# Cosformer attention followed by a low-rank mixer MLP: q features of four batches transposed by DMA, attention units moved to other PSUM banks

## The chip, the cores and the metric

The kernel runs on one core of a Trainium2 chip. The time is that of one execution on the device, in microseconds, taken on the slowest core, which here is the only one. The profiled execution is a single run with the hardware profiler; its span is the time from its first to its last instruction. TensorE (PE in the profile) multiplies matrices; what it writes goes to PSUM, which has eight banks of 128 partitions by 2 KB. VectorE (DVE) and ScalarE (ACT) read PSUM and write SBUF; GpSimd (POOL) converts v and issues the stores of the output; SyncE (SP) issues the loads and the DMA transposes.

## The reference

q, k and v have 8 batches, 8 heads, 576 positions and 64 features each, in float32. Attention is linear: no softmax, but features `phi`, a state `kv` per head, and a denominator. Its output is the input of a mixer with a low-rank part over the positions and an MLP over the channels.

```python
def phi(x, c, s):
    r = np.maximum(x, 0.0)
    return np.concatenate([r * c, r * s], axis=-1)       # 64 features become 128
q_p, k_p = phi(q, cos_w, sin_w), phi(k, cos_w, sin_w)    # cos_w, sin_w by position
kv = np.einsum('bhsf,bhsd->bhfd', k_p, v)
z = np.sum(k_p, axis=2)
num = np.einsum('bhsf,bhfd->bhsd', q_p, kv)
den = np.einsum('bhsf,bhf->bhs', q_p, z)[..., None] + 1e-06
attn = num / den

x = attn.transpose(0, 2, 1, 3).reshape(8, 576, 512)
h = x.transpose(0, 2, 1) @ U @ V                         # U 576 x 32, V 32 x 576
u = x + h.transpose(0, 2, 1)
out = u + np.maximum(u @ w_ch1, 0.0) @ w_ch2             # 512 -> 2048 -> 512
```

## The kernel before

**Tiling.** The 576 positions of a batch are cut into four chunks of 128 (chunk `c` holds positions 4p + c) and a tail of 64 (`c` = 4). Tails of an even and an odd batch share one tile, in its lower and upper 64 rows (`tail(b)`), so the MLP treats two batches as a pair with a common tail. All products are bf16.

**Attention of one batch** is a row of units:

- `k_prep`, `q_prep`, `v_prep`: k, q and v from the float32 loads to bf16 features, on DVE, ACT and POOL. The features of q of one batch stand in `q_p` (one buffer, four chunks of 128 rows by 8 heads x 128 features) and `q_tl`.
- `qtr_unit(b, c)` (L250): eight TensorE transposes, one for each head, turn one chunk of `q_p` so that features lie on partitions; they write a PSUM tile `t_ps` with tag `T` (one buffer), and one copy on DVE (in batches 2 and 3 sometimes ACT) brings it to `q_pT` (one buffer) or `q_tlT`.
- `kv_unit(b, hg)` (L229): the state of four heads, 20 matmuls, PSUM tag `T`, a cast on DVE.
- `x_unit(b, c)` (L311): eight matmuls of `q_pT` with `kv`, PSUM tag `X` (two banks), a reciprocal and a product on DVE, giving `x_bf`.
- `A_unit(b)` (L338): five matmuls with U, PSUM tag `T`, a cast on DVE; `u_unit(b, c)` (L354): one matmul with V, PSUM tag `T`, an addition on DVE, giving `u_bf` or `u_tl`.
- `utr_dma` (L377): DMA transposes of u, two chunks at a time (a 128 x 1024 matrix), and of the pair's tail (128 x 512), issued by SP; they write `uT` and `uT_tl`.

**The MLP of a pair** is 72 slots: 16 of `g1_main` for the even batch, 16 for the odd one (each four matmuls of 512 columns into tag `g`, three banks, and a ReLU on ACT), 4 of `g1_tail`, and 36 of `g2_part` (each four matmuls into tag `o`, two banks; after every fourth slot DVE adds u and POOL or SP issues the store). The four pairs make 288 slots, numbered through: pair 1, with batches 2 and 3, has slots 72 to 143, and its slots from 108 on are `g2_part`. `g1_main` of an even batch starts at slots 0, 72, 144, 216, that of an odd one at 16, 88, 160, 232.

**What sets the order.** Everything is written out by hand: each engine runs its instructions in the order in which the program issues them. After slot i the list `todo[i]` adds attention units. `attention_plan(b)` (L527) gives the slots of one batch relative to a slot `w`: preparation from `p0` on, `qtr_unit` at -9 to -1, `kv_unit` at 0 and 2, `x_unit` at 4 to 12, `A_unit` at 14, `u_unit` at 16 to 20, `utr_dma` at 18 to 21, and the loads of batch b + 1 at `p0` + 1, + 2 and + 7. `w` is 40, 57, 88, 124, 160 and 196 for batches 2 to 7. So the attention of batches 4 and 5 runs beside pair 1's MLP, that of 6 and 7 beside pair 2's, and pair 3's has none beside it. Batches 0 and 1 are ordered separately ahead of and beside the first slots.

SP's queue holds, in order, the loads (for each of k, v and q a tail of 128 KB and a main part of 1 MB; `kst` has two buffers, `vst` and `qst` one each) and the transposes of u. ACT's holds `q_prep` and the ReLUs of `g1_main`, so `q_prep` of batch 6 stands ahead of the ReLU of slot 144.

Of the kernel before, what the change touches and what calls it, by code (L numbers as in the profile page):

```python
# [17 lines left out]
def kernel(  # L18
# [11 lines left out]
    nc = tc.nc  # L30
# [18 lines left out]
    def tail(b):  # L49
        lo = TS * (b % 2)  # L50
        return slice(lo, lo + TS)
# [49 lines left out]
    def cast(eng, o, i):  # L101
        if eng is nc.scalar:
            nc.scalar.activation(out=o, in_=i, func=AF.Copy, bias=0.0, scale=1.0)
        else:
            eng.tensor_copy(out=o, in_=i)  # L105
# [140 lines left out]
    def qT_alloc(b):  # L246
        if b not in q_pT:
            q_pT[b] = pool.tile([P, 4, H, P], BF16, tag="q_pT", bufs=1, name="q_pT")

    def qtr_unit(b, c, h0=0, h1=H, eng=None, tag="T", bufs=1):  # L250
        qT_alloc(b)
        t_ps = ps.tile([P, H, P], BF16, tag=tag, bufs=bufs, name="t_ps")
        for h in range(h0, h1):
            nc.tensor.transpose(  # L254
                out=t_ps[:, h, :],
                in_=q_p[b][:, c, h, :] if c < 4 else q_tl[:, h, :],
                identity=ident,
            )
# [265 lines left out]

    ORD = (4, 0, 1, 2, 3)

    def attention_plan(b):  # L527

        p0 = -26 if b % 2 == 0 and b > 2 else -14
        plan = [(p0, lambda: v_prep(b))]  # L530
        for n, c in enumerate(ORD):
            ke = (V_, A_) if b == 3 else (V_, V_)
            plan.append((p0 + n, lambda c=c, ke=ke: k_prep(b, c, ke)))
            if b == 2:
                plan.append((p0 + n, lambda c=c: q_prep(b, c, (V_, A_))))
            else:
                plan.append((p0 + n, lambda c=c: q_prep(b, c, (A_, None))))
                plan.append((p0 + n + 1, lambda c=c: q_prep(b, c, (None, A_))))
            ev = A_ if b in (2, 3) and n % 2 == 0 else V_
            plan.append((-9 + 2 * n, lambda c=c, ev=ev: qtr_unit(b, c, eng=ev)))  # L540
        plan.append((0, lambda: kv_unit(b, 0, "T", 1)))
        plan.append((2, lambda: kv_unit(b, 1, "T", 1)))
        for n, c in enumerate(ORD):
            plan.append((4 + 2 * n, lambda c=c: x_unit(b, c, "X", 1)))
        plan.append((14, lambda: A_unit(b, "T", 1)))
        for n, c in enumerate(ORD):
            plan.append((16 + n, lambda c=c: u_unit(b, c, "T", 1)))
        if b % 2 == 1:
            plan.append((18, lambda: utr_dma(b, 4, 5)))
        plan.append((19, lambda: utr_dma(b, 0, 2)))  # L550
        plan.append((21, lambda: utr_dma(b, 2, 4)))
# [102 lines left out]
    def put(at, thunk):  # L654
        todo.setdefault(at, []).append(thunk)

    put(17, lambda: uTt_direct(0, "o", 2, V_))
    for n, (b, c) in enumerate([(b, c) for b in range(2) for c in ORD]):
        put(18 + n, lambda b=b, c=c: u_unit(b, c, "T", 1))
    for n, t in enumerate(loads(2, nc.sync)):  # L660
        put((11, 12, 12)[n], t)
    for b, w in ((2, 40), (3, 57), (4, 88), (5, 124), (6, 160), (7, 196)):
        for o, t in attention_plan(b):
            put(w + o, t)
    for i, s in enumerate(slots):
        s()
        for t in todo.get(i, []):
# [31 lines left out]
```

## Time and profile before

| | us |
|---|---|
| median of 3 runs (lowest to highest) | 354.38 (351.99 to 355.33) |
| the profiled execution's own time | 352.06 |
| its span | 350.3 |
| TensorE busy, share of the span | 326.5, 93% |
| DVE busy / ACT busy / POOL busy | 165.8 / 150.5 / 52.2 |
| first matmul of pair 1's `g2_part` (slot 108) | 165.95 |

The granted TensorE clock is 0.994 over the span. The page lists busy time by engine, the chain of work that ended last, and groups of instructions by line; answers of the trace give the same for a stretch of the span. A matmul's duration in a row contains its fill, and matmuls overlap: the distance between starts, which the chain of waits shows, is what one adds to TensorE's time. An idle time in brackets stands behind the instruction that waited, with what released it.

### The profile page before, as it was taken

The page shows a single profiled execution, that of the slowest core. Times are in us where ns is not written, and L with a number is a line of the kernel's source. Part 1 is how long each engine was busy: PE and PEld are TensorE (multiplying, and loading weights), DVE is VectorE, ACT ScalarE, POOL GpSimd, SP SyncE. Part 2 cuts the span into 40 slices and gives each one's busy share as a digit, 9 for nine tenths or more (in the row PEclk, how much of TensorE's full clock was granted, in tenths as well). Part 3 has the DMA queues.
Part 4 walks back from the last instruction along what each step waited for, and adds up shares of the span by engine and source line. Part 5 has one row for each costly group of instructions (what it writes and reads, how often), then busy time and mean ns, then how long its engine had stood idle before and what let it go on. Part 6 is the DMA issues. An engine that isn't in the chain of part 4 may idle for free.

```text
span 350.3 us, 6126 instructions
## 1 busy us (share of the span) xinstructions
PE 326.5 (93%) x2537; PEld 177.0 (51%) x2565; DVE 165.8 (47%) x355; ACT 150.5 (43%) x257; POOL 52.2 (15%) x101
## 2 busy tenths in 40 slices
PE   7689999999787899999999989999999999999995
PEld 2464654475444345556455435556455444464443
DVE  5668444845745953244745852244745630001211
ACT  2967445856627025565707025565600036660000
POOL 6340503003113040000111440000111100000000
PEclk9899999999999999999999999999999999999999
DMA  8999999964752993000798591000312150001121
GB/s 214 263 279 260 213 238 244 280 180 152 201 159 61 239 299 64 2 2 0 165 314 275 141 283 44 2 0 2 90 67 56 60 135 2 0 2 55 65 92 60
DMA packets 58587, 46.03 MB, mean 131 GB/s; under 512 B 26720, under 2 KB 55680, under 8 KB 58560
## 3 DMA queue, kind: packets, MB, share of 16 engines
q1 hardware_dynamic: 51856, 33.82, 37.9%
q0 software_dynamic: 6704, 11.82, 13.6%
q8 instruction: 20, 0.33, 0.4%
q14 instruction: 7, 0.06, 0.1%
HBM read 36.86 MB, written 9.44 MB: 132 GB/s over the span
## 4 chain that ended last, share of the span: by engine, by line
PE 75%; DVE 9%; DMA 9%; issue 3%; POOL 2%; ACT 1%; SPq 0%; POOLq 0%; DVEq 0%
PE o_ps L481 29%; PE g_ps L431 28%; DMA vst<-in_v_dram 5%; PE gt_ps L449 4%; PE t_ps L254 4%; PE va_ps L361 3%; DMA vt<-in_v_dram 3%; DVE k_p L205 3%; PE kv_ps L237 2%; DVE o_sb L491 2%; PE x_ps L318 2%; PE a_ps L344 2%; DMA w_bf<-in_moe_w_ch_dram 2%; POOL v_ext L105 1%; DVE u_bf L362 1%
## 5 line engine op out<-in xcount | busy, mean ns | idle before, releaser
L438 ACT ACTIVATE hid<-g_ps 128x512 bf16<-128x512 f32 x128 | 76.3, 597 | 116.9 <-PE g_ps L431 116.9
L431 PE MATMUL g_ps<-uT,w_bf 128*128 128x512 bf16 x512 | 120.6, 379 | 0.4
L481 PE MATMUL o_ps<-w_bf,hid 128*128 128x512 bf16 (+1 forms) x510 | 116.9, 372 | 1.4 <-DVE o_sb L491 0.5
L481 PEld LDWEIGHTS <-hid 128*128 128x128 bf16 x528 | 49.5, 98 | 52.6 <-issue 2.8
L431 PEld LDWEIGHTS <-w_bf 128*128 128x128 bf16 x512 | 47.9, 98 | 54.7 <-issue 4.8
L491 DVE TENSOR_TENSOR o_sb<-u_bf,o_ps 128x512 f32<-128x512 bf16 (+1 forms) x33 | 22.1, 669 | 61.6 <-PE o_ps L481 61.6
L501 POOL DMA_DIRECT2D out_dram<-o_sb x24 | 13.4, 558 | 180.9 <-DVE o_sb L491 164.4
L105 DVE COPY q_pT<-t_ps 128x1024 bf16<-128x1024 bf16 (+1 forms) x25 | 16.7, 668 | 26.5 <-PE t_ps L254 24.9
L362 DVE TENSOR_TENSOR u_bf<-x_bf,va_ps 128x512 bf16<-128x512 bf16 x32 | 22.0, 687 | 15.1 <-PE va_ps L361 15.1
L203 ACT ACTIVATE q_p<-qst,sinw 128x512 bf16<-128x512 f32 (+1 forms) x36 | 23.3, 664 | 0.0
L254 PE MATMUL t_ps<-ident,q_p 128*128 128x128 bf16 x256 | 20.4, 223 | 2.9 <-DVE q_pT L105 0.9
L254 PEld LDWEIGHTS <-q_p 128*128 128x128 bf16 x256 | 17.2, 99 | 9.7 <-issue 3.6
L105 POOL CAST v_ext<-vst 128x512 bf16<-128x512 f32 (+1 forms) x32 | 17.3, 582 | 17.7 <-DMA vst<-in_v_dram 16.1
L205 DVE TENSOR_SCALAR k_p<-kst,cosw 128x512 bf16<-128x512 f32 (+1 forms) x36 | 17.9, 514 | 1.6 <-DMA kst<-in_k_dram 1.6
L328 DVE TENSOR_TENSOR x_bf<-x_ps,rec 128x512 bf16<-128x512 f32 x24 | 16.6, 691 | 0.8
L361 PE MATMUL va_ps<-A_sb,V_bf 128*128 128x512 bf16 x39 | 14.7, 377 | 1.7 <-DVE u_tl L362 0.9
L449 PE MATMUL gt_ps<-uT_tl,w_bf 128*128 128x128 bf16 x256 | 16.1, 219 | 0.0
L449 PEld LDWEIGHTS <-w_bf 128*128 128x128 bf16 x256 | 15.1, 98 | 1.4
L237 PEld LDWEIGHTS <-k_p 128*128 128x128 bf16 x256 | 11.2, 98 | 8.3 <-issue 2.5
L203 ACT ACTIVATE q_p<-qst,cosw 128x512 bf16<-128x512 f32 x20 | 14.2, 710 | 2.4 <-DMA qst<-in_q_dram 2.4
L237 PE MATMUL kv_ps<-v_ext,k_p 128*128 128x65 bf16 x256 | 12.5, 195 | 2.9 <-DVE u_bf L362 1.9
L105 DVE CAST kv<-kv_ps 128x260 bf16<-128x260 f32 x16 | 6.8, 428 | 17.5 <-PE kv_ps L237 17.4
(95 smaller groups left out, 265.0 us busy)
## 6 DMA issues: line engine op xcount, KB each, us to landing
kst<-in_k_dram SPq DMA_DIRECT2D x7, 1024.0 KB, 11.2
qst<-in_q_dram SPq DMA_DIRECT2D x7, 1024.0 KB, 11.3
vst<-in_v_dram SPq DMA_DIRECT2D x7, 1024.0 KB, 11.3
out_dram<-o_sb POOLq DMA_DIRECT2D x24, 256.0 KB, 4.5
w_bf<-in_moe_w_ch_dram POOLq DMA_DIRECT2D x8, 512.0 KB, 11.8
out_dram<-o_sb SPq DMA_DIRECT2D x7, 256.0 KB, 2.3
kst<-in_k_dram SPq DMA_DIRECT2D x2, 512.0 KB, 7.7
qst<-in_q_dram SPq DMA_DIRECT2D x2, 512.0 KB, 8.8
```

Of the source, the lines that this page charges most:

```text
L105: eng.tensor_copy(out=o, in_=i)
L203: nc.scalar.activation(out=o, in_=i, func=AF.Relu, bias=0.0, scale=w)
L205: eng.tensor_scalar(out=o, in0=i, scalar1=0.0, scalar2=w, op0=ALU.max, op1=ALU.mult)
L237: nc.tensor.matmul(out=acc[:, i, :], lhsT=k_p[b][:, c, h, :] if c < 4 else k_tl[:, h, :], rhs=vx[:, c, h, :], start=(c == 0), stop=(c == 4),)
L254: nc.tensor.transpose(out=t_ps[:, h, :], in_=q_p[b][:, c, h, :] if c < 4 else q_tl[:, h, :], identity=ident,)
L361: nc.tensor.matmul(out=va, lhsT=V_bf[:, c, :], rhs=A_sb[b], start=True, stop=True)
L362: nc.vector.tensor_tensor(out=u_bf[b][:, c, :] if c < 4 else u_tl[b // 2][rows, :], in0=x_of(b, c, rows), in1=va[rows, :], op=ALU.add,)
L431: nc.tensor.matmul(out=g_ps.rearrange("p (c t) -> p c t", c=4), lhsT=w1_bf[:, d, j * P : j * P + P], rhs=uT[b][:, :, d, :], start=(d == 0) ...
L438: nc.scalar.activation(out=hid[b][:, j, :], in_=g_ps, func=AF.Relu, bias=0.0, scale=1.0)
L449: nc.tensor.matmul(out=g_ps[:, jj, :], lhsT=w1_bf[:, d, j * P : j * P + P], rhs=uT_tl[pr][:, d, :], start=(d == 0), stop=(d == 3),)
L481: nc.tensor.matmul(out=o[:, cols], lhsT=lhs[:, j, c * P : c * P + P], rhs=w2_bf[:, j, cols], start=(j == 0), stop=(j == NJ - 1),)
L491: nc.vector.tensor_tensor(out=o_sb[:, cols], in0=u[:, cols], in1=o[:, cols], op=ALU.add)
```

## The change: three parts

First, the q features of batches 4 to 7 are no longer transposed by `qtr_unit` but by a new function, `qtr_dma`: three DMA transposes for a batch, issued by SP. One turns the tail (64 rows by 1024), two turn two chunks each (128 x 2048). They write `q_pT` and `q_tlT` directly. The loads of the next batch, which stand in the same queue, get other slots: in batch 4 they are at -6 to -4, in batches 5, 6 and 7 (the last has none) at `p0` + 9 to + 11, behind the q transposes at `p0` + 4, + 6 and + 8.

Second, `kv_unit`, `A_unit` and `u_unit` of batches 2 to 7 (and `u_unit` of batches 0 and 1) leave tag `T`. They take tag `o` in the 36 slots of a pair in which `g1` runs, and tag `g` in those in which `g2` runs; `spare` makes the choice. Tag `T` is left to the q transposes of TensorE.

Third, in the part ahead of the first slot, `den_unit(0, 4, 8)` is issued ahead of one `xh_unit` and the two `uTd_open`, where it stood behind them.

The core of the diff:

```diff
+    def qtr_dma(b, c0, c1):
+        qT_alloc(b)
+        if c0 < 4:
+            nc.sync.dma_start_transpose(
+                out=q_pT[b][:, c0:c1, :, :].rearrange("f c h t -> f (c h) t"),
+                in_=q_p[b][:, c0:c1, :, :].rearrange("p c h f -> p (c h f)"),
+            )
+        else:
+            nc.sync.dma_start_transpose(
+                out=q_tlT[:, :, tail(b)],
+                in_=q_tl[tail(b), :, :].rearrange("p h f -> p (h f)"),
+            )
...
-    def attention_plan(b):
+    Q_BY_DMA = (4, 5, 6, 7)
+
+    def spare(at):
+        return ("o", 2) if at % 72 < 36 else ("g", 3)
+
+    def attention_plan(b, w):
+        plan = []
+
+        def put(at, f, *a, tag=False):
+            if tag:
+                a = a + spare(w + at)
+            plan.append((w + at, lambda: f(b, *a)))
...
-            ev = A_ if b in (2, 3) and n % 2 == 0 else V_
-            plan.append((-9 + 2 * n, lambda c=c, ev=ev: qtr_unit(b, c, eng=ev)))
-        plan.append((0, lambda: kv_unit(b, 0, "T", 1)))
-        plan.append((2, lambda: kv_unit(b, 1, "T", 1)))
+            if b not in Q_BY_DMA:
+                ev = A_ if b in (2, 3) and n % 2 == 0 else V_
+                put(-9 + 2 * n, qtr_unit, c, 0, H, ev)
+        lo = (p0 + 1, p0 + 2, p0 + 7)
+        if b in Q_BY_DMA:
+            q0 = (-18, -16, -8) if b == 4 else (p0 + 4, p0 + 6, p0 + 8)
+            for at, (c0, c1) in zip(q0, ((4, 5), (0, 2), (2, 4))):
+                put(at, qtr_dma, c0, c1)
+            lo = (-6, -5, -4) if b == 4 else (p0 + 9, p0 + 10, p0 + 11)
+        put(0, kv_unit, 0, tag=True)
+        put(2, kv_unit, 1, tag=True)
...
-        plan.append((14, lambda: A_unit(b, "T", 1)))
+            put(16 + n, u_unit, c, tag=True)
+        put(14, A_unit, tag=True)
...
-            for at, t in zip((p0 + 1, p0 + 2, p0 + 7), loads(b + 1, nc.sync)):
-                plan.append((at, t))
+            for at, t in zip(lo, loads(b + 1, nc.sync)):
+                plan.append((w + at, t))
...
-    for c in ORD[2:]:
+    for c in ORD[2:4]:
         xh_unit(0, c, 0, 4, rec0, "o", 2)
+    rec1 = den_unit(0, 4, 8, "X", 1)
+    xh_unit(0, 3, 0, 4, rec0, "o", 2)
     uTd_open(0, 0, "g", 3)
     uTd_open(0, 1, "g", 3)
-    rec1 = den_unit(0, 4, 8, "X", 1)
...
-        put(18 + n, lambda b=b, c=c: u_unit(b, c, "T", 1))
+        put(18 + n, lambda b=b, c=c: u_unit(b, c, *spare(18)))
```

How two queues read before and with the change, in the order in which the program issues them, where pair 1's MLP ends and pair 2's begins. First SP, in the kernel before, from the loads of batch 7 on; `uT_tl` is the tail of a pair (here of pair 2), `uT` two chunks of a batch (here of batch 5 twice, then of batch 6 twice):

```order
L81 DMA kt<-in_k_dram 64x8x64
L75 DMA kst<-in_k_dram 128x8x256
L81 DMA vt<-in_v_dram 64x8x64
L75 DMA vst<-in_v_dram 128x8x256
L81 DMA qt<-in_q_dram 64x8x64
L75 DMA qst<-in_q_dram 128x8x256
L386 DMA_TRANSPOSE uT_tl<-u_tl 128x4x128
L380 DMA_TRANSPOSE uT<-u_bf 128x8x128 x4
```

All six loads of batch 7 stand ahead of the transposes of batch 5's u. With the change, SP's queue reads at the same place, from the q transposes of batch 6 on:

```order
L272 DMA_TRANSPOSE q_tlT<-q_tl 128x8x64
L267 DMA_TRANSPOSE q_pT<-q_p 128x16x128
L399 DMA_TRANSPOSE uT_tl<-u_tl 128x4x128
L267 DMA_TRANSPOSE q_pT<-q_p 128x16x128
L393 DMA_TRANSPOSE uT<-u_bf 128x8x128
L81 DMA kt<-in_k_dram 64x8x64
L75 DMA kst<-in_k_dram 128x8x256
L81 DMA vt<-in_v_dram 64x8x64
L75 DMA vst<-in_v_dram 128x8x256
L393 DMA_TRANSPOSE uT<-u_bf 128x8x128
L81 DMA qt<-in_q_dram 64x8x64
L75 DMA qst<-in_q_dram 128x8x256
```

The loads of batch 7 have moved behind the q transposes of batch 6 and in between the transposes of u: the first half of batch 5's u stands ahead of k and v, the second half (chunks 2 and 3) behind them.

Second DVE, in pair 2's `g2_part` slots, where batch 7 is prepared; before, from the last feature of k of batch 7 to the cast of its state:

```order
L205 TENSOR_SCALAR k_p<-kst,sinw 128x8x64
L491 TENSOR_TENSOR o_sb<-u_bf,o_ps 128x512
L105 COPY q_tlT<-t_ps 128x8x64
L105 COPY q_pT<-t_ps 128x1024
L491 TENSOR_TENSOR o_sb<-u_bf,o_ps 128x512
L105 COPY q_pT<-t_ps 128x1024 x2
L491 TENSOR_TENSOR o_sb<-u_bf,o_ps 128x512
L105 COPY q_pT<-t_ps 128x1024
L105 CAST kv<-kv_ps 128x260 x2
```

With the change, at the same place:

```order
L205 TENSOR_SCALAR k_p<-kst,cosw 128x8x64
L205 TENSOR_SCALAR k_p<-kst,sinw 128x8x64
L504 TENSOR_TENSOR o_sb<-u_bf,o_ps 128x512 x3
L105 CAST kv<-kv_ps 128x260 x2
L504 TENSOR_TENSOR o_sb<-u_tl,o_ps 128x512
```

The five copies from `t_ps` are gone, and nothing stands between the last evictions `o_sb` and the state of batch 7. TensorE's order loses the eight transposes of each of these units in the same way and is otherwise unchanged from slot 0 on; ACT's and POOL's orders are the same as before.

More of the change, by code (lines that the diff above doesn't have):

```diff
@@ L534, in attention_plan @@
             if b == 2:
-                plan.append((p0 + n, lambda c=c: q_prep(b, c, (V_, A_))))
+                put(p0 + n, q_prep, c, (V_, A_))
             else:
-                plan.append((p0 + n, lambda c=c: q_prep(b, c, (A_, None))))
-                plan.append((p0 + n + 1, lambda c=c: q_prep(b, c, (None, A_))))
-            ev = A_ if b in (2, 3) and n % 2 == 0 else V_
-            plan.append((-9 + 2 * n, lambda c=c, ev=ev: qtr_unit(b, c, eng=ev)))
-        plan.append((0, lambda: kv_unit(b, 0, "T", 1)))
@@ L542, in attention_plan @@
-        plan.append((2, lambda: kv_unit(b, 1, "T", 1)))
+                put(p0 + n, q_prep, c, (A_, None))
+                put(p0 + n + 1, q_prep, c, (None, A_))
+            if b not in Q_BY_DMA:
[7 more added lines that the diff above has]
+            lo = (-6, -5, -4) if b == 4 else (p0 + 9, p0 + 10, p0 + 11)
@@ L543, in attention_plan @@
+        put(0, kv_unit, 0, tag=True)
+        put(2, kv_unit, 1, tag=True)
         for n, c in enumerate(ORD):
-            plan.append((4 + 2 * n, lambda c=c: x_unit(b, c, "X", 1)))
-        plan.append((14, lambda: A_unit(b, "T", 1)))
-        for n, c in enumerate(ORD):
-            plan.append((16 + n, lambda c=c: u_unit(b, c, "T", 1)))
+            put(4 + 2 * n, x_unit, c, "X", 1)
+            put(16 + n, u_unit, c, tag=True)
+        put(14, A_unit, tag=True)
         if b % 2 == 1:
-            plan.append((18, lambda: utr_dma(b, 4, 5)))
@@ L662 @@
     for b, w in ((2, 40), (3, 57), (4, 88), (5, 124), (6, 160), (7, 196)):
-        for o, t in attention_plan(b):
-            put(w + o, t)
+        for at, t in attention_plan(b, w):
+            put(at, t)
     for i, s in enumerate(slots):
```

10 lines of the change are left out of this document (5 added, 5 removed).

## The prediction

> **What bounds the kernel now.** I read the page first, then busy time by stage, then the chain of waits inside the stages.
>
> ```profile
> span 350.3 us, 6126 instructions
> PE 326.5 (93%) x2537; PEld 177.0 (51%) x2565; DVE 165.8 (47%) x355; ACT 150.5 (43%) x257; POOL 52.2 (15%) x101
> PE 75%; DVE 9%; DMA 9%; issue 3%; POOL 2%; ACT 1%; SPq 0%; POOLq 0%; DVEq 0%
> ```
>
> TensorE is busy for 93% of the span and carries three quarters of the chain that ended last. The next view gives, for a stretch of the span, its length and then the busy time of PE, PEld, DVE, ACT and POOL. The stretches are pair 0's second product, pair 1 and pair 2.
>
> ```profile
> 72.00:126.40 54.40, 46.39 (x413) 25.52 (x418) 32.46 (x69) 21.56 (x33) 10.83 (x20) 1.00 0.64 177
> 126.40:207.40 81.00, 79.09 (x600) 42.31 (x605) 43.96 (x91) 34.79 (x57) 12.06 (x22) 1.00 0.56 148
> 207.40:284.60 77.20, 76.53 (x590) 41.54 (x596) 36.55 (x75) 27.76 (x46) 8.17 (x15) 1.00 0.20 49
> ```
>
> In pairs 1 and 2, where batches 4 to 7 are prepared, TensorE idles 1.9 and 0.7 us: work taken from it there shortens the span, as long as nothing new comes late. Pair 0's second product has 8.0 us of idle time: there the waits count. DVE, the next busiest, has 40% or more of each stretch free.
>
> **The q transposes taken from TensorE.** The chain runs through them, in pair 2's first product like this (start, length, what):
>
> ```profile
> 213.40 0.45 PE t_ps L254 x8
> 213.84 1.73 PE g_ps L431 x8
> ...
> 222.09 0.45 PE t_ps L254 x8
> 222.54 0.86 PE g_ps L431 x4
> ```
>
> One unit of eight transposes adds 0.45 us between two slots. The change removes five units in each of four batches: 20 x 0.45 = 9.0 us. I take the chain's 0.45 us, not the duration of the group:
>
> ```profile
> L254 PE MATMUL t_ps<-ident,q_p 128*128 128x128 bf16 x256 | 20.4, 223 | 2.9 <-DVE q_pT L105 0.9 <-DVE A_sb L105 0.8 <-DVE u_tl L362 0.8
> L105 DVE COPY q_pT<-t_ps 128x1024 bf16<-128x1024 bf16 (+1 forms) x25 | 16.7, 668 | 26.5 <-PE t_ps L254 24.9 <-PE x_ps L318 1.4
> ```
>
> The 223 ns holds the fill, which overlaps the neighbour; 256 of them are 20.4 us busy together. The 20 copies to `q_pT` and `q_tlT` go from DVE as well, up to 20 x 0.67 = 13.4 us; DVE has that free, so I count nothing for it beyond the next part.
>
> **The shared bank.** Tag `T` has one buffer, so a unit that wants it waits until the unit before has been copied out. First the two places where the state of batch 5 and of batch 7 waited for the last q copy, and a unit that did not wait:
>
> ```profile
> 182.51 0.61 DVE q_pT L105
> 183.17 0.78 PE kv_ps L237 x20
> ...
> 185.67 0.60 PE kv_ps L237 x20
> ...
> 261.21 0.61 DVE q_pT L105
> 261.86 0.78 PE kv_ps L237 x20
> ```
>
> Each place costs 0.61 us and the 0.18 by which a restarted unit is longer: 1.6 us for both. Both the copy and the sharing go. Next TensorE's matmuls with the idle time ahead of them, in pair 0 and at the end of pair 1:
>
> ```profile
> 79.88 0.30 PE L237 MATMUL kv_ps<-v_ext,k_p 128*128 128x65 bf16 x4 [0.25 <-ACT q_pT L103]
> ...
> 95.99 0.61 PE L254 MATMUL t_ps<-ident,q_p 128*128 128x128 bf16 x8 [0.85 <-DVE q_pT L105]
> ...
> 100.19 0.61 PE L254 MATMUL t_ps<-ident,q_p 128*128 128x128 bf16 x8 [0.78 <-DVE A_sb L105]
> ...
> 103.51 0.61 PE L254 MATMUL t_ps<-ident,q_p 128*128 128x128 bf16 x8 [0.77 <-DVE u_tl L362]
> ...
> 105.22 0.38 PE L361 MATMUL va_ps<-A_sb,V_bf 128*128 128x512 bf16 x1 [0.25 <-ACT q_pT L103]
> 106.38 0.30 PE L237 MATMUL kv_ps<-v_ext,k_p 128*128 128x65 bf16 x4 [0.78 <-DVE u_bf L362]
> ...
> 110.48 0.28 PE L237 MATMUL kv_ps<-v_ext,k_p 128*128 128x65 bf16 x4 [1.08 <-DVE u_bf L362]
> ...
> 123.18 0.43 PE L318 MATMUL x_ps<-kv,q_pT 128*128 128x65 bf16 x8 [1.06 <-DVE x_bf L328]
> ```
>
> ```profile
> 203.21 0.38 PE L361 MATMUL va_ps<-A_sb,V_bf 128*128 128x512 bf16 x1 [0.87 <-DVE u_tl L362]
> ...
> 206.98 0.38 PE L361 MATMUL va_ps<-A_sb,V_bf 128*128 128x512 bf16 x1 [0.22 <-DVE u_bf L362]
> ```
>
> Six of pair 0's waits are between units of different kinds that shared `T`; with `kv`, `A` and `u` in the three idle `g` banks they end: 0.25 + 0.78 + 0.77 + 0.25 + 0.78 + 1.08 = 3.9 us. The 0.85 stays, one q unit waiting for another in batch 3, and so does the 1.06, which is `x_ps`. The two in pair 1 go too: 1.1 us. What could be late next in their place is DVE itself; at worst half of these 5.0 us comes back.
>
> The third part of the change, ahead of slot 0, I cost at nothing: slot 12 waits for the last piece of `w_ch1`, which lands at 44.6 (38.58 + 6.04 in the rows below), whatever TensorE did before. An earlier start waits there; a loss needs a start that is late by more than what TensorE waits there, and I bound it at 0.5 us, half a slot.
>
> ```profile
> 38.58 6.04 DMA w_bf<-in_moe_w_ch_dram
> 44.67 1.04 PE g_ps L431 x4
> ```
>
> Gains: 9.0 + 1.6 + 3.9 + 1.1 = 15.6 us.
>
> **What the DMA transposes cost.** They add 12 instructions to SP's queue and none to another engine. The nearest rows are the transposes of u (the last of them, 256 KB each, and the tail of 128 KB), and loads on the same queue; the last number is the time from issue to landing.
>
> ```profile
> uT<-u_bf SPq DMA_TRANSPOSE x2, 3.1
> uT_tl<-u_tl SPq DMA_TRANSPOSE x1, 2.5
> ```
> ```profile
> vst<-in_v_dram SPq DMA_DIRECT2D x1, 1024.0 KB, 11.3
> ...
> 203.18 1.27 SPq L386 DMA_TRANSPOSE uT_tl<-u_tl  x1
> ```
>
> Twice the size takes 0.6 us more, so a 512 KB transpose of q moves for about 2.4 us and lands after 3.1 + 1.2 = 4.3 us. Bounds: 3.1 us if it costs what 256 KB does, 6.2 us if all of it doubles. I take 4.3, by the slope of two sizes. SP is held 1.27 us by one (the upper bound for 512 KB is twice that). [...]
>
> Batches 4, 5 and 7 have time: their q features are issued 10 or more slots ahead of `x_unit`. The tight place is batch 6, where q, the rest of batch 5's u and the loads of batch 7 share SP's queue. I count T from the start of pair 1's second product.
>
> ```profile
> 165.95 0.81 PE o_ps L481 x3
> ...
> 169.89 0.60 SPq L81 DMA_DIRECT2D kt<-in_k_dram  x1
> ...
> 171.95 0.97 SPq L75 DMA_DIRECT2D vst<-in_v_dram  x1
> ...
> 187.79 0.72 ACT L203 ACTIVATE q_p<-qst,cosw 128x512 bf16<-128x512 f32 x1 [2.37 <-DMA qst<-in_q_dram]
> ...
> 192.10 0.71 ACT L203 ACTIVATE q_p<-qst,sinw 128x512 bf16<-128x512 f32 x1
> 202.46 0.69 DVE L362 TENSOR_TENSOR u_tl<-x_tl,va_ps 64x512 bf16<-64x512 bf16 x1
> ```
>
> The loads of batch 6 start at T = 3.9 before; behind three q transposes of batch 5 they start some 5 us later. So ACT finishes batch 6's q at T = 192.81 + 5 - 165.95 = 31.9. Slot 144 comes sixteen slots of 0.86 us ahead of slot 160's 50.2 (below), at 36.4, so the ReLUs queued behind do not wait. The tail of u (T = 37.2 before, less 2.2 for batch 5's five units and 0.8 for the wait at its state) is there at T = 34.2; its transpose, the second q transpose of batch 6 and one of u take SP to about 37.9. Then come k and v of batch 7. From the issue of batch 6's k to the landing of its v, issued at 171.95, took 171.95 + 11.3 - 169.89 = 13.4 us. Batch 5's last u transpose moves behind them for 1.2 us, so lands at T = 51.5 to 52.5. Its reader is slot 160, which began at 222.54, T = 56.6; less ten units (4.5), one restart (0.8) and two waits (1.1) it would begin at T = 50.2. TensorE waits about 1.7 us there. Bounds: 0, where the landing is 2 us earlier; 6, where a q transpose holds SP for 2.5 us and moves for twice my time. All of TensorE waits with slot 160, whose matmuls are next in its queue.
>
> Sum: span 350.3 - 15.6 + 1.7 = 336.4. The profiled execution took 352.06, 1.8 us more than its span, so 338.2; it lies 2.3 us under the median of the three runs, 354.38, which I carry over: **340.5 us**, with 336 to 344 for this case (waits come back, u's wait between its bounds). Chance 0.62.
>
> **Rivals.**
>
> *The queue jams more* (0.15). A q transpose takes twice what I count, in SP's issue and in movement. Its price is then 4 to 8 us more at slot 160: 344.5 to 348.5. For it: 512 KB is not in the trace, nor rows of 64 to be turned. Against: a transpose of 128 KB and one of 256 KB differ little.
>
> *Only the matmuls go* (0.09). DVE, which is late at 123.18, is as late in the places where `T` was: only 9.0 + 1.6 - 1.7 us are gained, 345.5. Against: DVE has 22 us free in pair 0's second product.
>
> *The transposes were cover* (0.05). What is removed filled waits for DVE, the 1.06 us kind, and half of the 9.0 us is lost too: about 350. Against: pairs 1 and 2 have 2.6 us of idle time in all.
>
> *Slower than before: ACT and TensorE blocked by slow transposes* (0.07). The place is batch 6 again. If each 512 KB transpose takes x us longer, batch 6's loads come 2x later, and so does ACT's `q_prep`, which stands ahead of slot 144's ReLU; batch 6's own q transposes add 2x before k, v and the last u of batch 5. Slot 160 then waits about 4x longer, less some 2 us for which the queue waits for u now. From x = 4 us the 15.6 are gone; at x = 5 the time is 340.5 + 18 = 358. It needs 6.4 us of movement for 512 KB against the 2.4 of the rows. [...]
>
> *The transposes cost more than the chain shows* (0.02). At 223 ns each, the row's duration, 160 would free 36 us: 316. [...] Against: eight pass in 0.45 us, 56 ns each.
>
> **How the numbers follow.** A comparison here can tell about 1% from no change, 3.5 us. Faster by more than that (under 350.8): the forecast, the jam, "only the matmuls", the 316 and half of "cover", 0.90; same: the other half and a little of the slow case, 0.05; slower: 0.05. The range takes the forecast's own 336 to 344, 345.5, and more than half of the jam, to 347; below, no wait at slot 160 and a median as close to the profile as the lowest run, 335. It leaves out under 0.2.
>
> **What would show it.** TensorE's `t_ps` group at 160 matmuls fewer, four slots of pair 2's first product back to back where 0.45 us lay between; pair 1 near 74.7 us and pair 2 near 71.8 plus the wait. No wait of `kv_ps`, `t_ps` or `va_ps` behind another kind of unit in 95 to 111. A wait of TensorE on a DMA at slot 160, 0 to 6 us long; ACT's batch 6 q ready ahead of slot 144. I am wrong if a transpose of q lands after more than 6.2 us with the queue empty, if DVE is named where `T` was, or if the gap at slot 160 is over 6 us.

## The result, and the profile after

The changed kernel takes 342.49 us in the median of four executions (337.59 to 342.88), the kernel before 354.11 us (351.99 to 355.33) in the same comparison. Two of these four and one of two more took over 1.5% longer than the fastest of them; without such executions, as in every median and ratio from here on, the changed kernel takes 340.27 us, a ratio of 0.961 with a 95% interval of 0.951 to 0.971. The forecast was 340.5 us, with 335 to 347 for the range. The profiled execution took 337.59 us; 338.2 had been worked out for it. A second comparison of the same kernel (below) gave 340.15 us.

The page of the kernel after, in the lines that answer to those shown of before: span, busy time by engine, and the chain of work that ended last.

```profile
span 335.8 us, 5846 instructions
PE 316.6 (94%) x2405; PEld 168.9 (50%) x2405; DVE 154.2 (46%) x335; ACT 150.4 (45%) x257; POOL 53.1 (16%) x101
PE 82%; DVE 8%; DMA 5%; issue 2%; SPq 1%; ACT 1%; POOL 0%; DVEq 0%; POOLq 0%
```

The span is 14.5 us shorter, TensorE's busy time 9.9 us: about a third of the gain came out of idle time. Busy time by stage (columns as before: stretch, length, PE, PEld, DVE, ACT, POOL) shows where. The stretches of before are pair 1's first product, its second product, and pair 2's first sixteen slots up to slot 160:

```profile
126.41:165.95 39.54, 39.43 (x327) 22.17 (x326) 16.23 (x33) 21.18 (x36) 3.39 (x6) 1.00 0.23 54
165.95:205.73 39.78, 38.20 (x268) 19.55 (x273) 26.52 (x57) 13.01 (x21) 7.88 (x14) 1.00 0.85 235
205.73:222.54 16.81, 16.59 (x107) 8.69 (x106) 4.38 (x7) 9.38 (x16) 3.44 (x6) 1.00 0.42 79
```

The same stages after:

```profile
121.43:158.16 36.73, 36.73 (x288) 19.98 (x286) 13.03 (x27) 21.09 (x36) 3.40 (x6) 1.00 0.58 142
158.16:194.85 36.69, 35.92 (x235) 17.53 (x234) 24.05 (x52) 13.10 (x21) 8.62 (x14) 1.00 0.90 214
194.85:211.51 16.66, 14.03 (x65) 6.17 (x63) 1.79 (x3) 9.55 (x16) 1.51 (x3) 1.00 1.08 252
```

Pair 1's first product is 2.8 us shorter, its second 3.1. The last stage hardly moved, 16.81 to 16.66, though TensorE's work in it fell from 16.59 to 14.03, above all by its five `t_ps` units: as much is now idle. The waits of TensorE after (us in total, times, longest) say what ended that:

```profile
PE g_ps L444 <- DMA uT<-u_bf: 2.6, 1, 2.6
...
PE t_ps L254 <- DVE q_pT L105: 0.9, 1, 0.9
PE a_ps L357 <- DVE x_bf L341: 0.8, 1, 0.8
```

The first row is new. The waits of before between units of tag `T` (`kv_ps` behind `u_bf`, `t_ps` behind `A_sb` and `u_tl`, `va_ps` behind `u_tl`) are gone; the 0.9 of one q unit for another stayed. The chain and, behind it, SP's queue show the new wait at its place, ahead of slot 160:

```profile
202.79 8.68 DMA uT<-u_bf
...
211.51 1.04 PE g_ps L444 x4
212.55 0.60 PE kv_ps L237 x20
```
```profile
197.96 1.66 SPq L393 DMA_TRANSPOSE uT<-u_bf  x1
199.67 0.61 SPq L81 DMA_DIRECT2D kt<-in_k_dram  x1
...
201.74 0.95 SPq L75 DMA_DIRECT2D vst<-in_v_dram  x1
202.79 4.81 SPq L393 DMA_TRANSPOSE uT<-u_bf  x1
```

The last transpose of batch 5's u is issued behind k and v of batch 7 and lands 8.7 us later. The group of q transposes on TensorE fell by 128 instructions (chunks) in this row, and by 32 (tails) in another:

```profile
L254 PE MATMUL t_ps<-ident,q_p 128*128 128x128 bf16 x128 | 10.4, 224 | 1.5 <-DVE q_pT L105 0.9 <-ACT q_tlT L103 0.7
```

### The profile page after: what moved, and what is told of

Its sections match the earlier page's. It is cut to its first block, busy times and chain, and to the rows that moved or that the text cites. A ratio compares the mean times of both kernels' runs of the same rounds, so it can differ in the third digit from the quotient of the medians.

```text
span 335.8 us, 5846 instructions
## 1 busy us (share of the span) xinstructions
PE 316.6 (94%) x2405; PEld 168.9 (50%) x2405; DVE 154.2 (46%) x335; ACT 150.4 (45%) x257; POOL 53.1 (16%) x101
## 4 chain that ended last, share of the span: by engine, by line
PE 82%; DVE 8%; DMA 5%; issue 2%; SPq 1%; ACT 1%; POOL 0%; DVEq 0%; POOLq 0%
PE o_ps L494 33%; PE g_ps L444 29%; PE gt_ps L462 4%; PE kv_ps L237 3%; PE t_ps L254 3%; DMA uT<-u_bf 3%; PE va_ps L374 3%; PE a_ps L357 2%; DMA qt<-in_q_dram 2%; DVE k_p L205 2%; PE x_ps L331 2%; PE w_ps L173 1%; DVE o_sb L504 1%; DVE k_tl L205 1%; DVE x_bf L341 1%
## 5 line engine op out<-in xcount | busy, mean ns | idle before, releaser
L444 PE MATMUL g_ps<-uT,w_bf 128*128 128x512 bf16 x512 | 119.1, 379 | 2.9 <-DMA uT<-u_bf 2.6
L494 PE MATMUL o_ps<-w_bf,hid 128*128 128x512 bf16 (+1 forms) x528 | 118.2, 372 | 0.5 <-DVE o_sb L504 0.5
L375 DVE TENSOR_TENSOR u_bf<-x_bf,va_ps 128x512 bf16<-128x512 bf16 x32 | 21.9, 687 | 10.2 <-PE va_ps L374 10.2
L494 PE MATMUL o_ps<-w_bf,hid_tl 128*128 128x512 bf16 x64 | 15.4, 379 | 0.0
L331 PEld LDWEIGHTS <-q_pT 128*128 128x128 bf16 x192 | 9.0, 98 | 9.7 <-DVE x_bf L341 3.7
L103 ACT ACTIVATE q_pT<-t_ps 128x512 bf16<-128x512 bf16 (+1 forms) x11 | 8.4, 789 | 12.0 <-PE t_ps L254 8.2
L331 PE MATMUL x_ps<-kv,q_pT 128*128 128x65 bf16 x192 | 10.1, 194 | 3.0 <-DVE x_bf L341 3.0
```

The lines of the kernel that those rows point to most:

```text
L331: nc.tensor.matmul(out=acc[:, g, i * E : i * E + E], lhsT=qT_of(b, c, h), rhs=kv_sb[b][:, h, :], start=True, stop=True,)
L375: nc.vector.tensor_tensor(out=u_bf[b][:, c, :] if c < 4 else u_tl[b // 2][rows, :], in0=x_of(b, c, rows), in1=va[rows, :], op=ALU.add,)
L444: nc.tensor.matmul(out=g_ps.rearrange("p (c t) -> p c t", c=4), lhsT=w1_bf[:, d, j * P : j * P + P], rhs=uT[b][:, :, d, :], start=(d == 0) ...
L494: nc.tensor.matmul(out=o[:, cols], lhsT=lhs[:, j, c * P : c * P + P], rhs=w2_bf[:, j, cols], start=(j == 0), stop=(j == NJ - 1),)
```

## The experiments

The theory to be tested: the gain is the sum of 20 `t_ps` units at 0.45 us, two restarts and eight waits at tag `T`, less one wait at slot 160 for a transpose of u that stands behind loads. The rivals: the q transposes themselves are slow and block SP's queue; the gain sits in the banks alone; the new order of the start costs something. The first four kernels that follow, without the one marked otherwise, ran on one chip, with 353.04 us for the kernel before. "The first profile" is that of the changed kernel, shown above.

### The banks alone

```diff
-    Q_BY_DMA = (4, 5, 6, 7)
+    Q_BY_DMA = ()
```

> The new PSUM tags and the new place of den_unit alone: all q transposes on TensorE, the loads in their old slots. Theory (TensorE is the bound; shared bank and transposes add up): the waits behind units of another kind go, 3.9 us in pair 0 and 1.1 in pair 1, and the 1.6 at the states of batches 5 and 7; the nine us of transposes stay: span 343.7 to 345.3, about 350.3 less 5.0 to 6.6. Rival (the bank was all, and transposes only filled waits): span within 1.5 us of the changed kernel's 335.8. Rival 2 (DVE takes the place of the bank): span over 348.

Measured: 343.36 us (342.71 to 343.88), ratio 0.974 (0.971 to 0.976), span 340.9. The banks are worth 9.4 us of span, not the 5.0 to 6.6 that the waits shown as idle add up to; the span is below the 343.7 to 345.3 expected. Those waits are gone from the list, so they are in it; some 2.8 us came from where the profile shows no idle time. The place is where u units follow each other, as in slots 18 to 27, with `u_unit` of batches 0 and 1. TensorE and then DVE in the kernel before:

```profile
57.59 0.38 PE L361 MATMUL va_ps<-A_sb,V_bf 128*128 128x512 bf16 x1
57.80 1.02 PE L431 MATMUL g_ps<-uT,w_bf 128*128 128x512 bf16 x4
58.74 0.38 PE L361 MATMUL va_ps<-A_sb,V_bf 128*128 128x512 bf16 x1
```
```profile
58.00 0.69 DVE L362 TENSOR_TENSOR u_bf<-x_bf,va_ps 128x512 bf16<-128x512 bf16 x1 [0.47 <-PE va_ps L361]
```

TensorE again, with the banks alone changed:

```profile
57.22 0.38 PE L374 MATMUL va_ps<-A_sb,V_bf 128*128 128x512 bf16 x1
...
58.30 0.38 PE L374 MATMUL va_ps<-A_sb,V_bf 128*128 128x512 bf16 x1
```

Before, one `va_ps` and the next lie 1.15 us apart, now 1.08. In between the one buffer goes round: the matmul (0.41 to DVE's start), DVE's addition (0.69, to 58.69), and 0.05 to the next `va_ps`, 1.15 us in all. The work of a slot with its u unit is five matmuls of 0.216, 1.08 us. So each of these u units waited 0.07 us for the one before, and no idle time is listed, since the `g_ps` row ahead of it reaches to 58.82 with its fill. There are 40 u units: 40 x 0.07 = 2.8 us. That is an estimate with 0.07 as the mean: elsewhere in the trace of before most u units have 0.04 to 0.08, the first of a batch mostly none, and one that starts again after a listed wait up to 0.16. A run of its own tests it.

### The banks alone, but u stays in tag T

This one ran later, on another chip (the kernel before: 352.24 us).

```diff
-            put(16 + n, u_unit, c, tag=True)
+            put(16 + n, u_unit, c, "T", 1)
...
-        put(18 + n, lambda b=b, c=c: u_unit(b, c, *spare(18)))
+        put(18 + n, lambda b=b, c=c: u_unit(b, c, "T", 1))
```

> Edit: the bank part alone (no DMA transposes of q), with u_unit of all batches put back on tag T (one buffer) and only kv_unit and A_unit in the idle g and o banks. Theory (what the bank part gained beyond the 6.6 us of waits that the profile showed lies in u_unit: with one buffer a va_ps takes 0.29 us of the chain instead of 0.22, 40 times, though nothing is shown as idle): the 40 units give 40 x 0.07 = 2.8 us back, and the waits for or of u units come back (t_ps behind u_tl 0.77, va_ps behind q_pT 0.25, and 0.87 + 0.22 in pair 1): 2.1 us. Span 340.9 + 4.9 = 345.8 (345 to 346.5); va_ps 0.28 to 0.29 each in the chain in slots 18 to 27. Rival (the surplus lies in kv_unit and A_unit, or in DVE's order): only the waits come back, span 342.5 to 343.5, va_ps 0.22 in the chain.

Measured: 348.25 us (347.36 to 348.97), ratio 0.988 (0.985 to 0.991), span 345.6; `va_ps` takes 0.28 to 0.29 us in the chain again. That is 4.7 us of span more than with u in the idle banks, against 4.9 expected. So half of what the banks bring comes from `u_unit` alone, and more than half of that from a wait that the profile doesn't list.

### The DMA transposes alone

```diff
-        return ("o", 2) if at % 72 < 36 else ("g", 3)
+        return ("T", 1)
```

> The DMA transposes and the new slots of the loads alone: kv, A and u units of every batch on tag T as before (and den_unit in its new place). Theory: 9.0 us of transposes and the 1.6 at the states of batches 5 and 7 go, 2.6 come as the wait at slot 160, and the 3.9 and 1.1 us of waits for T stay: span about 342 (341 to 344). Rival (the transposes were cover for DVE): span 346 to 350.

Measured: 344.76 us, ratio 0.978 (0.975 to 0.982), span 342.6. TensorE's waits, in the rows that matter:

```profile
PE g_ps L444 <- DMA uT<-u_bf: 1.9, 1, 1.9
PE kv_ps L237 <- DVE u_bf L375: 1.9, 2, 1.1
...
PE a_ps L357 <- DVE x_bf L341: 1.0, 1, 1.0
```

The prediction's terms for this part make 9.0 + 1.6 - 1.9 = 8.7; it brought 7.7. The wait of `a_ps` for DVE is 1.0 us, where before had 0.3: 0.7 of the missing 1.0. (The ReLU of slot 16 comes 0.5 us earlier here than in the kernel before, so behind it the gain is 7.2, and what else is missing isn't traced.) Neither part is the whole: 9.4 and 7.7, less the 1.6 for the restarts at the states of batches 5 and 7 that each of them removes, are 15.5, against 14.5 in the first profile, where the wait at slot 160 is 0.7 longer.

### The old order ahead of slot 0

```diff
-    for c in ORD[2:4]:
+    for c in ORD[2:]:
         xh_unit(0, c, 0, 4, rec0, "o", 2)
-    rec1 = den_unit(0, 4, 8, "X", 1)
-    xh_unit(0, 3, 0, 4, rec0, "o", 2)
     uTd_open(0, 0, "g", 3)
     uTd_open(0, 1, "g", 3)
+    rec1 = den_unit(0, 4, 8, "X", 1)
```

> The changed kernel with den_unit(0, 4, 8) back in its old place. Theory (costs nothing): slot 0 starts within 0.5 us of the changed kernel's 28.30 where TensorE's clock rises at the same time, and the span is 335.8 within 0.7. Rival (the reorder made the start 1.2 us later, 28.30 against 27.10): slot 0 starts near 27.1, and by slot 16 at least 0.5 us of it is left, span 335.3 or less.

Measured: 340.77 us, ratio 0.967 (0.963 to 0.971), span 338.7. No difference from the changed kernel can be told (its two medians are 340.27 and 340.15), so the order of the start costs nothing that shows. Slot 0 began at 27.48 us, between the 28.30 and 27.06 of the changed kernel's two profiles: the start varies more by itself. The span missed the 335.8 that was expected, because this profile had something new at slot 160. Busy time in short stretches; the third number from the end is the granted TensorE clock:

```profile
210.00:212.00 2.00, 0.40 (x1) 0.13 (x2) 0.00 (x0) 0.00 (x0) 1.37 (x3) 0.63 1.03 206
212.00:216.00 4.00, 4.00 (x28) 2.16 (x27) 0.43 (x1) 0.60 (x1) 1.53 (x3) 0.50 0.73 230
216.00:220.00 4.00, 4.00 (x36) 2.02 (x35) 0.43 (x1) 1.79 (x3) 0.00 (x0) 0.83 0.00 0
```

TensorE waited 3.4 us here, and then ran at half clock. In the first profile of the changed kernel the gap was 2.6 us and the clock stayed at 1.00. This was tested next but one.

### The loads of batch 7 behind both transposes of batch 5's u

```diff
             lo = (-6, -5, -4) if b == 4 else (p0 + 9, p0 + 10, p0 + 11)
+            if b == 6:
+                lo = (p0 + 12, p0 + 13, p0 + 14)
```

> The changed kernel with one edit: the loads of batch 7 go from slots 143 to 145 to slots 146 to 148, so that both transposes of batch 5's u stand ahead of them in SP's queue. Theory (SP's queue order makes TensorE wait at slot 160): the 2.6 us wait of g_ps on the DMA of uT is gone, nothing takes its place, the span is 333.2 us where the changed kernel has 335.8, the time about 0.8% lower. Rival 1 (the transposes are slow in themselves there, whatever stands ahead): the wait stays above 1.5 us. Rival 2 (the loads of batch 7 become late instead): a wait of DVE, ACT or POOL for kst, qst or vst of batch 7 in pair 2's g2 slots, and a span of 335.8 or more.

Measured: 335.32 us (334.73 to 336.01), ratio 0.950 (0.948 to 0.953), span 333.2. TensorE runs through slot 160 (at 209.80 its next unit):

```profile
195.99 13.98 PE L444 MATMUL g_ps<-uT,w_bf 128*128 128x512 bf16 x64
209.80 0.29 PE L237 MATMUL kv_ps<-v_ext,k_p 128*128 128x65 bf16 x4
```

The wait is gone with the place in the queue, and nothing waits for the later loads. So it is the order of SP's queue, as the prediction had it, that costs the wait; the q transposes, which are the same here, can stay. A second run of this kernel gave 334.54 us.

### The changed kernel again, and the gap filled with matmuls

The next four share another chip (the kernel before: 353.11 us). First the changed kernel itself, to see its gap and clock a second time.

> The changed kernel itself, once more, beside the next one. Theory (the gap at slot 160 lasts 2.5 to 3.5 us; in executions where it is over some 3 us the granted clock falls to 0.5 for several us behind it, and the execution is 2 to 4 us longer than its gap explains): times of 337.5 where the clock stays, 340 to 343 where it falls, and a mean granted clock of 0.98 to 0.985 with the longer ones. Rival (the spread has nothing to do with the gap): no relation of time and clock.

Measured: 340.15 us (339.78 to 340.45), ratio 0.961 (0.954 to 0.968), span 338.6. The chain at slot 160, first here, then in the first profile:

```profile
202.89 8.53 DMA uT<-u_bf
...
211.47 1.89 PE g_ps L444 x4
213.35 1.10 PE kv_ps L237 x20
214.46 3.27 PE g_ps L444 x8
...
230.03 1.03 PE a_ps L357 x4
```
```profile
213.16 1.73 PE g_ps L444 x8
...
227.14 1.08 PE a_ps L357 x5
```

The transpose landed at the same time, 211.42 and 211.47. Here TensorE had come 0.8 us earlier and waited 3.4 us; four matmuls then took 1.89 us instead of 1.04, twenty of `kv_ps` 1.10 instead of 0.60, eight 3.27 instead of 1.73. By `a_ps` it is 2.9 us behind the first profile, about the 2.8 by which the spans differ. The granted clock is nearly that of the run with the old start: 0.66 in 210 to 212, 0.50 in 212 to 216, 0.82 in 216 to 220, so about 6.8 us at half clock (1.36 + 4 + 1.44). In this program arriving earlier at the gap made the end later.

Then ten matmuls of zeros (128x512, to a `T` tile that nobody reads) behind slot 159, for a shorter gap:

```diff
+    put(159, lambda: keep_warm(10, "T", 1))
```

> The changed kernel with ten matmuls on zeros (128x512, 2.2 us) behind slot 159, which TensorE runs while the last u transpose of batch 5 is on its way. They feed nothing. Theory (the gap lets the clock fall): the granted clock stays at 1.00 behind slot 160, the profiled time stays at 337.5 to 338.5 and so do the other executions, 2 to 5 us under the changed kernel's median. Rival (the clock falls for another reason, or the transpose is what costs): the median is that of the changed kernel, or 2.2 us more.

Measured: 340.06 us (339.74 to 342.87), ratio 0.963 (0.956 to 0.970). TensorE's wait at slot 160 was 1.2 us and the clock 1.00 throughout that stage, as expected, but the time was not below the changed kernel's. The profiled execution had lost time ahead of slot 16 (a wait of 2.9 us for a piece of `w_ch1`, with the clock at 0.5 from 47.9 to 51.3 us; its ReLU of slot 16 is at 58.37, against 52.86 in the run above). From that ReLU to the end it took 341.1 - 58.4 = 282.7 us, the run above 338.6 - 52.9 = 285.8. A second profile, on another chip (the kernel before: 352.87 us), shows whether it was the start that ate the gain:

> The kernel with ten matmuls of zeros behind slot 159, a second time, one profiled run. In its first profile the stretch from the ReLU of slot 16 to the end took 282.7 us, against 285.8 where the clock had fallen behind the gap; but its time was not below that kernel's, because the start lost some 5 us to a late piece of w_ch1. Theory (the start varies by itself, behind slot 16 nothing does): 282 to 283.5 us from the ReLU of slot 16 to the end again, clock 1.00 at slot 160, and whatever the time is above 338.5 is lost ahead of slot 16. Rival (the gain at slot 160 is given back behind it): over 284 us behind slot 16 with a start like that of the changed kernel.

Measured: 339.31 us, span 337.5. The ReLU of slot 16 is at 54.10, so 283.4 us lie behind it: inside the 282 to 283.5 expected. The granted clock around the gap (TensorE waits 2.0 us in the first of them):

```profile
210.00:214.00 4.00, 2.04 (x10) 0.80 (x9) 0.00 (x0) 0.00 (x0) 1.73 (x4) 1.00 1.20 253
214.00:218.00 4.00, 4.00 (x55) 2.46 (x54) 0.86 (x2) 1.79 (x3) 1.17 (x2) 1.00 0.63 200
```

In the profiles, then, a shorter gap averts the fall of the clock and saves 2.4 to 3.1 us behind slot 16 against the profile in which it fell. It is no better than a gap without a fall: the first profile, without the zeros, took 282.0 us there. That the median did not follow stays open: the unprofiled runs leave only a time and a mean clock, and two of the changed kernel's here have 340.06 and 340.24 at 0.99 and 0.995, too high for a fall of 6.8 us (about 0.01 of the mean) beside the one that each start has. What they lost instead isn't known.

### The q transposes of batches 5 and 6 doubled

```diff
+            if b in (5, 6):
+                spare_T = pool.tile([P, 2, H, P], BF16, tag=f"spare{c0}", bufs=1, name="spare_T")
+                nc.sync.dma_start_transpose(
+                    out=spare_T.rearrange("f c h t -> f (c h) t"),
+                    in_=q_p[b][:, c0:c1, :, :].rearrange("p c h f -> p (c h f)"),
+                )
```

> The changed kernel with each of the four 512 KB q transposes of batches 5 and 6 issued a second time into a tile that nothing reads. Theory (batch 6 is the tight place: what those transposes take longer comes back at slot 160, two of them by way of batch 6's loads and ACT, two in the queue ahead of k, v and the last u): with 2.5 to 3.5 us for each, TensorE's waits between slots 144 and 160 are 2.6 + 10 to 14 us long, and the span 346 to 351. Rival (SP's queue has room there, the wait is only that one transpose behind two loads): span 336 to 341.

Measured, one execution: 353.63 us, span 351.9. TensorE's waits:

```profile
PE g_ps L450 <- DMA uT<-u_bf: 8.2, 1, 8.2
PE g_ps L450 <- ACT hid L457: 4.1, 1, 4.1
```

This is the mechanism of the prediction's slower rival, at the place it named: ACT is still at batch 6's `q_prep` when slot 144's ReLU is due, TensorE stops for 4.1 us, and again for 8.2 at slot 160. The two waits are 12.3 us, a little under what was expected, and the span is above its 346 to 351: a wait of 2.6 us for `w_ch1` and two falls of the clock (0.57 in 203 to 207 us, 0.50 in 224 to 228) came on top. That there was room left in the queue for twice the bytes is refuted. The rival's "from x = 4 us" isn't far off: with the four transposes of these two batches doubled the whole gain is gone.

### No stores beside the transposes

```diff
+        if pr in (1, 2):
+            return
         eng = nc.sync if pr == NPAIR - 1 else nc.gpsimd
```

> The changed kernel without the stores of pairs 1 and 2 (left out: the output of batches 2 to 5). In the changed kernel the q transposes of batches 5 and 7 landed after 5.4 to 7.1 us and held SP for 2.5 to 3.6, where those of batch 4, beside which no store ran, took 4.3 and 1.9. Theory (stores from POOL's queue on the same DMA engines slow them): 4.2 to 4.6 us each, SP held under 2.2, and the wait at slot 160 under 2 us. Rival (two in a row, or the reads of q_p while ACT writes, slow them): landings of batches 5 and 7 stay above 5.3.

Measured, one execution: 339.51 us, span 337.7 (2.5 us of it a wait for `w_ch1` at the start). SP's queue at the q transposes of batch 5, in the first profile of the changed kernel and then here, with the time that SP was held:

```profile
161.34 1.21 SPq L272 DMA_TRANSPOSE q_tlT<-q_tl  x1
163.08 6.93 SPq L267 DMA_TRANSPOSE q_pT<-q_p  x2
```
```profile
165.04 1.20 SPq L272 DMA_TRANSPOSE q_tlT<-q_tl  x1
166.78 4.52 SPq L267 DMA_TRANSPOSE q_pT<-q_p  x2
```

And the issues of the same stretch (160 to 175 us) with their median time to landing, in the same order:

```profile
out_dram<-o_sb POOLq DMA_DIRECT2D x4, 256.0 KB, 5.0
q_pT<-q_p SPq DMA_TRANSPOSE x2, 6.7
```
```profile
q_pT<-q_p SPq DMA_TRANSPOSE x2, 5.5
```

Without the stores two transposes hold SP for 4.5 us instead of 6.9 and land after 5.5 instead of 6.7; the wait at slot 160 was 1.6 us. One by one, the first of the two now lands after 4.4 us (7.0 with the stores), the second after 6.5 (6.3). So stores on POOL's queue slow them, but only by a part: the second of two in a row is late without them too. Nor does each store do so: batch 4's first transpose had parts of two stores beside it (117.3 to 119.9 and 121.4 to 124.0 us) and took 4.26 us.

### The q features of batch 3 by DMA as well

To see whether a removed unit is worth the same in a stage where TensorE also waits for DVE, and beside the kernel with the loads moved, on the chip with 352.24 us for before:

> The kernel with the loads of batch 7 behind all transposes of batch 5's u, a second time, as the measure for the next run on the same chip. Span 333.2 (332.5 to 334.5), TensorE waits for no u transpose, no clock under 0.9 after 30 us.

Measured: 334.54 us, ratio 0.950 (0.946 to 0.953), span 334.0.

```diff
-    Q_BY_DMA = (4, 5, 6, 7)
+    Q_BY_DMA = (3, 4, 5, 6, 7)
...
+            if b == 3:
+                q0 = (p0 + 6, p0 + 10, p0 + 11)
...
+            if b == 3:
+                lo = (p0 + 1, p0 + 2, p0 + 7)
```

> Edit: as the run before, and the q features of batch 3 go by DMA as well, behind the loads of batch 4's k and v in SP's queue. Theory (a removed unit is worth its 0.45 us of chain wherever the transpose has time): 5 x 0.45 = 2.25 us, and the 0.85 us wait of one q unit for another goes; nothing new is late. Span 330 to 331.5 against 333.2. Rival (the stretch around batch 3 in pair 0's second product is bound by DVE's products x_bf and by SP's queue, so that x_unit of batch 3 waits for q_pT): span 333 or more, with a wait of x_ps on a DMA of q_pT or on x_bf that is longer than before.

Measured: 332.31 us (331.81 to 333.1), ratio 0.943 (0.940 to 0.945), span 330.8: 2.2 us under the kernel with the loads moved by the medians and 3.2 by the spans, against 2.25 + 0.85 = 3.1. Of the 3.2, 0.65 lies ahead of slot 16, where nothing was changed. The stage itself, from slot 16 to slot 72, took 65.9 us, and 68.8 in both profiles of the kernel with the loads moved: 2.9 us. The wait of `t_ps` behind `q_pT` is gone from the list, and those of `x_ps` behind `x_bf` are 3.2 us in all, against 3.0: DVE's pace there hides little of the gain. This is the fastest version of the study.

## Why the prediction was right, and where its terms were off

**The sum.** The removed work was costed rightly. Twenty units at 0.45 us: five more of the kind brought, with one 0.85 us wait, 2.9 us in their stage, where the same price gives 3.1. At 223 ns a matmul (the 316 us rival, which with the other terms of the sum would have been near 314) five units would have brought 9 us.

**The shared bank: mis-sized.** The term "0.25 + 0.78 + 0.77 + 0.25 + 0.78 + 1.08", 1.1 for pair 1 and 1.6 for the restarts, 6.6 us, took what the profile shows as idle. Measured alone the banks bring 9.4. The difference is mostly in the units of u, 0.07 us for each of 40 in the mean: a buffer's round trip of 1.15 us where the slot has 1.08 us of work. I priced the waits that are listed, and did not set the round trip of a single buffer against the spacing of its units. "Only the matmuls go" (345.5, where DVE is late in place of `T`) falls with that, but a little of it is there: `a_ps` waits 0.8 us for DVE, against 0.3 before, and pair 1's second product gave 3.1 us, where 3.9 were forecast (2.2 + 0.8 + the 0.87 at 203.21).

**The wait at slot 160: the mechanism was right, its size low.** It was where it had been put, for the transpose that had been named, and moving the loads removes it. It was 2.6 and 3.4 us in two profiles, against 1.7 in bounds of 0 and 6. The step that was off is the price of a 512 KB transpose. "Lands after 3.1 + 1.2 = 4.3 us" held where no other of its kind stands next to it in the queue: batch 4's two take 4.26 and 4.37 us, batch 6's first 4.28. Batch 6's second, issued 3.8 us behind the first (194.70, 190.94) with the tail of u between them, takes 6.5. Batch 5's two, one behind the other and beside stores, take 7.04 and 6.28, and hold SP for 3.2 and 3.6 us where I had 1.27 with 2.5 as the upper bound. So the loads of batch 6 started 11.9 us into pair 1's second product and not some 5 us after 3.9. ACT finished batch 6's q at T = 35.2, not 31.9:

```profile
192.66 0.71 ACT L203 ACTIVATE q_p<-qst,sinw 128x512 bf16<-128x512 f32 x1
195.75 0.60 ACT L451 ACTIVATE hid<-g_ps 128x512 bf16<-128x512 f32 x1 [2.39 <-PE g_ps L444]
```

That leaves 2.4 us ahead of slot 144's ReLU; the doubled transposes used them up. The transpose of u landed at T = 211.47 - 158.16 = 53.3 where 51.5 to 52.5 was forecast, and TensorE arrived at 50.7 (211.51 - 2.6 - 158.16), for 50.2. That the landing came out within 2 us is in part luck: k of batch 7 was issued at T = 41.5 (199.67), 3.6 us behind the 37.9 of the forecast, but from there to the landing of v took 10.7 us and not 13.4. "The queue jams more" was thus right about its cause, for batch 5 over twice the time in issue and about twice in movement, and wrong about the price: an added wait of 1 to 2 us and not 4 to 8, because ACT had room for its part and the loads were quicker.

At best, the slope of the sizes held in the first profile: 128 KB landed after 2.4 us, 256 KB after 3.1 and 512 KB after 4.3, so each 128 KB add about 0.6 us, by which, as an estimate, 512 KB move in about 2.4 us.

**What the profiled time stood for.** 338.2 was forecast for the profiled execution, and 337.59 measured. The terms, put in with what they measured, are 9.0 + 1.6 + 5.0 + 2.8 for u, less 2.6 at slot 160, 0.5 for `a_ps` and 0.55 for a start that was later by that much at slot 16 (53.85, 53.30 before; 52.86 in the changed kernel's second profile, so this is the spread of the start): 14.75, and the span fell by 14.5. So two errors nearly cancelled: 2.8 us too little for the banks, and some 2 us too little for DMA, DVE and start.

**Carrying 2.3 us to the median** came out close for a reason that I did not have. The median is 2.7 us above this profile in the first comparison: the other two executions counted have a mean clock of 0.98 and 0.985, against 0.99. In the second, the profiled execution is at the median, and its span is 2.8 us longer because the clock fell behind the gap. That step, "All of TensorE waits with slot 160", lacked what the wait does to the clock: a gap of 3.4 us cost 3.4 + 2.9 us. It explains the profiles; not every unprofiled run, as said above.

**The start** costs nothing that shows, as forecast, and "the transposes were cover" (350) falls: the transposes alone take 344.76. The slower rival needed twice the bytes in the queue.

## What to carry to other kernels

When work moves from an engine to a DMA queue, write down what stands behind it in that queue and who needs each item first, and let transfers that nobody needs soon go last: moving three loads by three slots was worth about 5 us here. Look for the cost of a shared single buffer not only in listed waits but by setting its round trip (producer, reader, and back) against the spacing of the units. And a gap of TensorE can cost more than its length: where the clock fell behind one of 3.4 us, it cost another 2.9.

## What the runs showed of the hardware that was not expected

**The clock behind a gap.** At slot 160, gaps of 3.36 and 3.40 us were followed by a granted clock of 0.5 for about 6.8 us; after 1.2, 1.6, 1.9, 2.0 and 2.6 us it stayed at 1.00. In the run with doubled transposes it fell at both gaps, of 4.1 and 8.2 us. But the length alone does not decide. Ahead of slot 16, where TensorE waited for a piece of `w_ch1`, gaps of 2.55 us (the run without stores) and 2.90 us (the first with zeros) had a fall of 3.4 us, and one of 2.58 us (doubled transposes) had none.

All six falls of these five profiles begin a whole number of times 3.41 us (9, 55, 57 or 60) after the clock's rise at 15 to 17 us; 3.41 us is also the length of the fall at the start of the kernel before (11.59 to 15.00 us). So the traces can be cut into windows of 3.41 us from that rise on. Here are the two windows that share the gap of 2.6 us at slot 160 in the first profile, then, from the run without stores, the window that ends with the fall and the next one (length, TensorE's busy time, and third from the end the clock):

```profile
206.69:210.11 3.42, 2.19 (x11) 0.78 (x8) 0.00 (x0) 2.02 (x4) 0.00 (x0) 1.00 1.16 311
210.11:213.52 3.41, 2.00 (x27) 1.30 (x28) 0.32 (x1) 0.60 (x1) 2.91 (x5) 1.00 1.13 284
```
```profile
43.68:47.09 3.41, 1.25 (x20) 0.77 (x18) 2.62 (x5) 0.60 (x1) 0.00 (x0) 1.00 1.14 242
47.09:50.51 3.42, 3.03 (x15) 1.36 (x16) 0.68 (x1) 0.60 (x1) 0.00 (x0) 0.50 1.17 248
```

The six windows that end with a fall hold 0 to 1.25 us of TensorE's work; in all profiles, up to 325 us, every other window at full clock holds at least 1.85 (2.00 in the first profile, at 210.11, and 2.25 in that of the kernel before, at 86.68). What counted is thus how much of a gap lay in one window, and the gap of 2.6 us was cut in two by luck. This is read from the profiles; no run was made to test it.

The falls last one, two or three times 3.41 us: 3.41 at the start of the kernel before, 6.83 at that of the first profile (12.13 to 18.96 us), and about 10.2 behind the gap of 8.2 us (a clock of 0.53 in 220 to 224, 0.50 in 224 to 228 and 0.69 in 228 to 232 us). A window that ends with a fall need not be wholly idle: that of the run without stores holds 1.25 us of work, and its gap was 2.55 us.

**Transposes in a queue.** A DMA transpose of 512 KB (128 rows by 2048) landed after 4.3 to 4.4 us in the three cases with no other of that size next to it in the queue or still on its way when it was issued, 5.5 us in the median of two in a row, and 6.7 us of two with 256 KB stores from another queue beside them; SP is held 1.8 to 2.0 us by the first kind and 3.2 to 3.6 by the last. One of 256 KB, which lands after 3.1 us elsewhere, held SP for 4.8 us and landed after 8.7 behind two 1 MB loads.

**A wait that no list shows.** Where a matmul's row, with its fill, reaches over a short wait of the next one, the wait is counted as busy: 0.07 us for a unit of u in slots 18 to 27, and some 2.6 us in all (the 4.7 us of span that u in tag `T` costs, less the 2.1 of listed waits).
